# A field step between us and h in units 2 to 21, four more units with the second product in halves, and another order of w_out's splits

## The chip, the cores and the metric

The kernel runs on one core of one Trainium2 chip. The metric is the device time of one execution, in microseconds (us), of which the median over the runs is given. Engines are named as in the profile: PE is TensorE's matmuls and PEld its weight loads, DVE is VectorE, ACT ScalarE, POOL GpSimd, SP SyncE (here the queue that issues DMAs).

## What is computed

```python
X = np.fft.fft(np.fft.fft(x, axis=1), axis=2).real     # x: (8, 3008, 256), float32
h = X.reshape(24064, 256) @ w_in                        # w_in: (256, 2048)
g = np.where(h >= 1, h, np.where(h <= -1, 0.0, (h + 1) ** 2 / 4))
out = g @ w_out                                         # w_out: (2048, 256)
```

The weights arrive as 64-bit floats and are made into float32 on the chip.

## The kernel before

**Units.** The second axis of the transform is folded into w_in, so that the rest is two matrix products with the function g between them. They are cut into 384 units: a batch (8), a chunk of columns (3, of 482, 512 and 512 columns) and 128 of the 2048 hidden features. Each unit carries two signs, since a column and its mirror image come from the same two products. Batch 0 runs its first four features for all three chunks (units 0 to 11), and then the other twelve, chunk by chunk. Units 12 to 23 are features 4 to 15 of the first chunk, 482 columns wide.

**One unit i.** `gemm1(i)` puts six matmuls into two banks `uv` (line 552; three banks in all). DVE adds a correction to the first, giving `us` (line 555). It then writes the difference and the sum with the second bank into a tile `h` (lines 558 and 559, tag `h`, four buffers). ACT makes `a` from `h` (lines 564 and 565). One iteration later `activate` has DVE make g from `a` and `h` (line 574 or 579), and some iterations later `gemm2` multiplies it into four `acc` banks (line 635). From unit 12 on, `gemm2(i)` stands in iteration i + 4.

**Native units and units in halves.** Units below `NATIVE` keep g as one float32 tile in the tag `gh`, and `gemm2` takes four float32 products of it with `wo32` (eight matmul records in the trace, since each product is recorded as two). From `NATIVE` on, g is written over `h`, ACT copies it to a rounded tile `gh` (line 582), and POOL subtracts the two into `gl` (line 598, two instructions, one for each sign). `gemm2` then takes three products per bank, twelve in all, with w_out's high half `woh` and low half `wol`. `low_halves(i)` issues `gl` at the end of iteration i + 2. The first of its two instructions waits for the DVE instruction whose name stands in `after[1]`: the last g, or the last low half of w_out on DVE if one was issued since. In units of this kind the tile `h` is read until `gl` is done.

**The conversions.** Sixteen pieces of the weights (0 to 15) are converted between the units. The step names are: A takes the mantissa field (line 253) and B the exponent field (line 258), both on DVE, and `a` is the two together; b is three ACT instructions (lines 267 to 269); c is two DVE instructions (lines 274 and 275); d is a multiplication on POOL (line 289). Pieces 2, 3, 6, 7, 10, 11, 14 and 15 are w_out's q = 0 to 7, two features each. u takes the high half of one q on ACT (line 300); O takes its low half on DVE (line 304) and Q on POOL. Of the rest, s is the low half of w_in (DVE, lines 363 and 368), f its folding on PE, L loads a part of batch 1's x, and Y folds one on POOL (line 153). A conversion works in a tile of two fields whose tag `WORK` gives, `h` where it names none. Tiles of one tag share its buffers: a new tile takes one only when all readers of an older tile are done.

**Order.** `AHEAD[i]` names steps between `us` and `h` of unit i, `AMID[i]` steps behind `h`, and `STEPS[i]` steps at the end of iteration i (before `gemm2`, if they stand ahead of a "|"). In iterations 0 to 23 `pin()` fixes the order of every engine to the order of the program, so that an instruction that waits holds up everything behind it on its engine. Iterations 22 and 23 hold the first two column sums of batch 1 on PE (`stage1`), which read what Y0 and Y1 have folded.

Of the kernel before, what the change touches and what calls it, by code (L numbers as in the profile page):

```python
# [11 lines left out]
U32 = mybir.dt.uint32  # L12
# [10 lines left out]
P = 128  # L23
# [5 lines left out]
CH = 512  # L29
# [12 lines left out]
def _constants():  # L42
# [36 lines left out]
)  # L79
AHEAD = {1: "v2 G0"}  # L80
AMID = {0: "p11", 1: "p12 D1 E1 q11 q12", 3: "p13 q13", 6: "p14 q14", 7: "f2", 11: "f4", 16: "f6"}
STEPS = {
    0: "c2",
    1: "b3",
    2: "c3 d3",
    3: "a4 b4",
    4: "a5 c4 d4 b5",
    5: "c5 d5",
    7: "f3 a8 s2 b8",
    8: "s3 r1 a9 c8 d8 b9",  # L90
    9: "a6 c9 d9 b6",
    10: "c6 d6",
    11: "f5 a12 s4 b12",
    12: "s5 r2 a13 c12 d12 b13",
    13: "a7 c13 d13 b7",
    14: "c7 d7 u0",
    15: "a10 b10 L0 L1 u1 Q0",
    16: "s6 u2 Q1 |",
    17: "f7 a11 c10 d10 b11",
    18: "s7 r3 c11 d11 L2",  # L100
    19: "a14 Y0 b14 L3 u3 O2",
    20: "a15 c14 d14 b15",
    21: "O3 c15 d15 u4",
    22: "O4 Y1 u6 u5",
    23: "O6 O5 u7",
    24: "O7",
    32: "h",
}

RAW = {0: "gh", 1: "gh", 2: "woh", 3: "woh", 4: "woh", 5: "woh", 6: "wol", 7: "wol", 8: "wol", 9: "wol"}  # L110
RAW |= {10: "xt", 11: "xt", 12: "xt", 13: "xt", 14: "pqh", 15: "pql"}
WORK = {1: "a", 3: "a", 4: "gl", 5: "gl", 7: "a", 8: "gl", 9: "gl", 11: "a", 12: "gl", 13: "gl", 15: "a"}
BUFS = {"h": 4, "a": 3, "gl": 4}

EARLY_BANKS = 12
BANK = {"s2_0_3": "acc3", "delta_1": "acc2"}
FIRST = 4
NATIVE = 20
PINNED = 24
SPARE = (3, 5)  # L120
NEXT = 22
# [5 lines left out]
def fft_ffn_kernel(ctx: ExitStack, tc: tile.TileContext, x, xn, cst, w_in, w_out, out):  # L127
# [3 lines left out]
    sb = ctx.enter_context(tc.tile_pool(name="sb", bufs=1))  # L131
# [3 lines left out]
    xt, yt, zt, nyb, pq = {}, {}, {}, {}, {}  # L135
# [90 lines left out]
    raws, f32s, wo32, shared = {}, {}, {}, {}  # L226
# [20 lines left out]
    def convert_mantissa(n):  # L247
        raw = raws.pop(n)
        tag = WORK.get(n, "h")
        t = sb.tile([P, 2, CH], U32, tag=tag, name=f"cv_{n}", bufs=BUFS[tag])  # L250
        high = raw[:, :, 1]
        cv[n] = t, raw
        nc.vector.tensor_scalar(t[:, 0], high, 0xFFFFF, None, op0=ALU.bitwise_and)  # L253
# [6 lines left out]
    def convert_fields(n):  # L260
        convert_mantissa(n)
        convert_exponent(n)
# [14 lines left out]
    def convert_scale(n, eng):  # L277
        t, _ = cv.pop(n)
        kind, q, *_ = jobs[n]
        man, exp = (t[:, i].bitcast(F32) for i in range(2))  # L280
        dst = man
        if kind == "in":
            f32s[n] = man
        else:
            if q % 2 == 0:
                pair = sb.tile([P, 2, CH], F32, tag="gl", name=f"wo_{q // 2}", bufs=4)
                wo32[q], wo32[q + 1] = pair[:, 0], pair[:, 1]
            dst = wo32[q]
        eng.tensor_tensor(dst, man, exp, op=ALU.mult)  # L289

    wo = {}
# [78 lines left out]
    s1, s2, zn = {}, {}, {}  # L370
# [172 lines left out]
    def gemm1(i):  # L543
# [11 lines left out]
        nc.vector.scalar_tensor_tensor(us, nyb[b, k][:, :n], delta[:, f : f + 1], uv[0], op0=ALU.mult, op1=ALU.add)  # L555
        run_steps(AHEAD.get(i, ""))
        h = sb.tile([P, 2, CH], F32, tag="h", name=f"h_{i}", bufs=4)[:, :, :n]
# [11 lines left out]
    def activate(i):  # L569
        n = WIDTH[units[i][1]]  # L570
        h, a = fronts.pop(i)
        if i < NATIVE:
            g = sb.tile([P, 2, CH], F32, tag="gh", name=f"g_{i}", bufs=4)[:, :, :n]
# [38 lines left out]
    def gemm2(i):  # L612
# [8 lines left out]
        for dh in range(2):  # L621
# [4 lines left out]
            for sg in range(2):  # L626
                acc = accs[dh * 2 + sg]
                if i < NATIVE:
                    wo_at = (f % 2) * D + dh * P
# [45 lines left out]
    def piece_sums(n):  # L675
# [21 lines left out]
        "q": lambda n: stage2_split(0, n - n1 - 1),  # L697
        "a": convert_fields,
        "A": convert_mantissa,
        "B": convert_exponent,  # L700
        "b": convert_floats,
        "c": convert_join,
        "d": lambda n: convert_scale(n, nc.gpsimd),
        "v": lambda n: convert_scale(n, nc.vector),
        "F": lambda n: fold_half(n, 0),
        "f": fold_w_in,
# [13 lines left out]
    def run_steps(names):  # L720
        for s in names.split():
            steps[s[0]](int(s[1:] or 0))
# [17 lines left out]
    for i in range(n_units + LAG):  # L740
# [29 lines left out]
        if i < n_units:  # L770
            run_steps(then)
            change = units[i][2] == (FIRST if b == 0 else 0) + LAG
            while pending and (change or units[i][2] != (FIRST if b == 0 else 0) + LAG - 1 and done < total * (r + 1 - r0) / (per - r0)):
                change = False
                w, f = pending.pop(0)
                f()
                done += w
                n = XC if b + 1 < PLAIN else XT
# [92 lines left out]
```

## Time and profile before

| | us |
|---|---|
| median of 3 runs | 1712.52 |
| lowest and highest of them | 1712.27, 1714.09 |
| the profiled execution | 1712.49 |
| its span, first to last instruction | 1710.7 |

In the profile PE is busy for all but 5.6 us of the span, DVE for 79%, ACT for 78% and POOL for 66% of it. The granted clock of TensorE is full in every slice. The page gives each engine's busy time; the chain of work names what the end of the span hangs on; a timeline lists one engine's instructions in order of time, with the idle time before each in brackets.

### The profile page before, as it was taken

To read this page: it belongs to the slowest core of one execution; us is meant where nothing else is said; L and a number is where in the kernel's file an instruction comes from. 1 tells how busy PE (TensorE), PEld (TensorE's weight loads), DVE (VectorE), ACT (ScalarE), POOL (GpSimd) and SP (SyncE) were. 2 spreads that over 40 slices of the span, in tenths; PEclk is the share of its full clock that TensorE was granted. 3 is DMA by queue.
4 is the path that set the end of the run, shared out by engine and by line. 5 is a ranking of instruction groups with operands and counts; after the bars stand their busy time and mean duration, and the time that the engine had idled before them with its cause. 6 is when DMAs were issued, how large, how long until landed. Compare 5 with 4: busy or idle time off the path is not lost.

```text
span 1710.7 us, 21453 instructions
## 1 busy us (share of the span) xinstructions
PE 1705.1 (100%) x7736; PEld 1389.1 (81%) x7736; DVE 1353.6 (79%) x1762; ACT 1335.6 (78%) x1541; POOL 1123.2 (66%) x921
## 2 busy tenths in 40 slices
PE   9999999999999999999999999999999999999999
PEld 6557888888888888888888888888888888888887
DVE  8998788877777787777777778777777777778776
ACT  6878777877788777887787877887778877777775
POOL 1125678856887568865688657886577855566664
PEclk9999999999999999999999999999999999999999
DMA  8123111100011000110010100101001010000000
GB/s 322 48 98 109 59 57 56 61 13 31 25 45 60 20 25 25 56 48 20 25 62 20 59 8 25 62 24 56 19 13 62 1 36 31 1 25 24 1 25 25
DMA packets 35466, 76.29 MB, mean 45 GB/s; under 512 B 4640, under 2 KB 13344, under 8 KB 35360
## 3 DMA queue, kind: packets, MB, share of 16 engines
q1 hardware_dynamic: 35180, 74.79, 12.6%
q8 instruction: 61, 1.00, 0.2%
q14 instruction: 45, 0.37, 0.1%
q10 hardware_dynamic: 180, 0.14, 0.0%
HBM read 47.10 MB, written 27.81 MB: 44 GB/s over the span
## 4 chain that ended last, share of the span: by engine, by line
PE 99%; DMA 0%; DVE 0%; SPq 0%; ACT 0%; issue 0%
PE acc L635 62%; PE uv L552 31%; PE s L509 3%; PE s L391 2%; PE s L396 1%; PE wps L342 1%; DMA raw<-in_moe_w_in_dram 0%; PE delta L321 0%; PE ny L482 0%; DVE cv L289 0%; DVE o L653 0%; DVE cv L275 0%; DVE y L153 0%; DVE cv L274 0%; DVE o L641 0%; DVE cv L253 0%
## 5 line engine op out<-in xcount | busy, mean ns | idle before, releaser
L598 POOL TENSOR_TENSOR gl<-h,gh 128x512 fp32r<-128x512 f32 (+1 forms) x724 | 908.9, 1276 | 449.2 <-PE acc L635 220.2
L564 ACT ACTIVATE a<-h,biases 128x1024 f32<-128x1024 f32 (+1 forms) x385 | 436.0, 1133 | 265.6 <-DVE h L559 264.1
L635 PE MATMUL acc<-gh,woh 128*128 128x512 f32 (+1 forms) x1456 | 574.3, 394 | 0.0
L635 PE MATMUL acc<-gl,woh 128*128 128x512 f32 (+1 forms) x1456 | 570.0, 391 | 0.0
L635 PE MATMUL acc<-gh,wol 128*128 128x512 f32 (+1 forms) x1456 | 566.9, 389 | 0.0
L555 DVE SCALAR_TENSOR_TENSOR us<-nyb,delta,uv 128x512 f32<-128x512 f32 (+1 forms) x384 | 282.9, 737 | 287.9 <-PE uv L552 287.3
L579 DVE SCALAR_TENSOR_TENSOR h<-a,h 128x1024 f32<-128x1024 f32 (+1 forms) x365 | 477.2, 1308 | 2.6 <-ACT a L565 2.1
L582 ACT ACTIVATE gh<-h 128x1024 fp32r<-128x1024 f32 (+1 forms) x365 | 379.8, 1040 | 46.6 <-DVE h L579 29.5
L565 ACT ACTIVATE a<-a 128x1024 f32<-128x1024 f32 (+1 forms) x385 | 395.1, 1026 | 1.1
L635 PEld LDWEIGHTS acc<-gl,woh 128*128 128x128 f32 x1456 | 274.3, 188 | 57.1
L635 PEld LDWEIGHTS acc<-gh,wol 128*128 128x128 f32 x1456 | 273.7, 188 | 56.4
L635 PEld LDWEIGHTS acc<-gh,woh 128*128 128x128 f32 x1456 | 273.8, 188 | 53.5
L552 PE MATMUL uv<-pqh,wh 128*128 128x512 f32 (+1 forms) x768 | 306.3, 399 | 0.0
L558 DVE TENSOR_TENSOR h<-us,uv 128x512 f32<-128x512 f32 (+1 forms) x384 | 260.3, 678 | 52.0 <-DVE us L555 1.5
L552 PE MATMUL uv<-pql,wh 128*128 128x512 f32 (+1 forms) x768 | 299.3, 390 | 0.0
L552 PE MATMUL uv<-pqh,wl 128*128 128x512 f32 (+1 forms) x768 | 298.9, 389 | 0.0
L559 DVE TENSOR_TENSOR h<-us,uv 128x512 f32<-128x512 f32 (+1 forms) x384 | 257.5, 671 | 0.0
L552 PEld LDWEIGHTS uv<-pqh,wl 128*128 128x128 f32 x768 | 144.2, 188 | 35.0 <-issue 4.6
L552 PEld LDWEIGHTS uv<-pqh,wh 128*128 128x128 f32 x768 | 144.2, 188 | 33.4 <-issue 3.6
L552 PEld LDWEIGHTS uv<-pql,wh 128*128 128x128 f32 x768 | 144.1, 188 | 30.2 <-DVE pql L220 0.4
L166 POOL TENSOR_TENSOR x<-x 120x256 f32<-120x256 f32 x72 | 68.2, 948 | 4.6 <-DVE h L579 3.5
L635 PE MATMUL acc<-g,wo 128*128 128x482 f32 (+1 forms) x160 | 69.6, 577 | 0.0
(80 smaller groups left out, 783.5 us busy)
## 6 DMA issues: line engine op xcount, KB each, us to landing
x<-in_xn_dram SPq DMA_DIRECT2D x36, 512.0 KB, 3.5
out_dram<-o SPq DMA_DIRECT2D x26, 512.0 KB, 2.8
x<-in_x_dram SPq DMA_DIRECT2D x16, 512.0 KB, 6.1
out_dram<-o SPq DMA_DIRECT2D x14, 482.0 KB, 2.9
nyb<-nyr SPq DMA_DIRECT2D x24, 256.0 KB, 3.2
raw<-in_moe_w_in_dram SPq DMA_DIRECT2D x4, 512.0 KB
raw<-in_moe_w_out_dram SPq DMA_DIRECT2D x4, 512.0 KB, 10.5
part<-o SPq DMA_DIRECT2D x4, 512.0 KB, 3.0
```

The costliest lines, as they stand in the source:

```text
L166: return nc.gpsimd.tensor_tensor(t[:, r], t[:, r], t[:, r + 1], op=ALU.add).ins
L509: nc.tensor.matmul(pt[:, i], z[:, c], rm, start=True, stop=True)
L552: nc.tensor.matmul(t[:, :n], w[m][:, cols], r[:, m, :n], start=(j == 0), stop=(j == 2))
L555: nc.vector.scalar_tensor_tensor(us, nyb[b, k][:, :n], delta[:, f : f + 1], uv[0], op0=ALU.mult, op1=ALU.add)
L558: nc.vector.tensor_tensor(h[:, 0], us, uv[1], op=ALU.subtract)
L559: last_h = nc.vector.tensor_tensor(h[:, 1], us, uv[1], op=ALU.add).ins
L564: nc.scalar.activation(a[:, sg], h[:, sg], AF.Relu, bias=half, scale=0.5)
L565: nc.scalar.activation(a[:, sg], a[:, sg], AF.Square)
L579: g = nc.vector.scalar_tensor_tensor(h[:, sg], a[:, sg], 1.0, h[:, sg], op0=ALU.min, op1=ALU.max).ins
L582: nc.scalar.activation(gh[:, sg], h[:, sg], AF.Copy)
L598: ins = nc.gpsimd.tensor_tensor(gl[:, sg], h[:, sg], gh[:, sg].bitcast(F32), op=ALU.subtract).ins
L635: nc.tensor.matmul(acc[:, :n], w, g[:, sg], start=(begin and j == 0), stop=(last and j == len(terms) - 1))
```

## The change

`AHEAD` gets one field step (A or B) for 18 of the units 2 to 21, between `us` and `h`; these steps stood in pairs at the ends of iterations. `NATIVE` falls from 20 to 16, so that units 16 to 19 (features 8 to 11) take three products per bank instead of one. These features need q = 4 and 5 of w_out in halves, so O4 stands in iteration 18 and O5 in 20 (before 22 and 23), O6 in 22 and O7 in 24, and O2 and O3 move behind them, to 25 and 26. Q0 moves from iteration 15 to 14 and Q1 from 16 to 15. For q = 4 to 7, `wo32` is no longer a tile of its own in the tag `gl` but the conversion's own tile, which is thus read until u and O of that q are done. The conversions' tiles move: pieces 9, 12 and 13 share the tag `z`, 10 takes `xt`, 14 takes `a`, and 11 and 15, now named in no entry, take `h`.

```diff
-AHEAD = {1: "v2 G0"}
+AHEAD = {
+    1: "v2 G0",
+    2: "A4",
+    3: "B4",
+    4: "A5",
+    5: "A8",
+    6: "B8",
+    7: "A9",
+    8: "B9",
+    9: "A6",
+    10: "A7",
+    11: "A12",
+    12: "A13",
+    13: "B13",
+    14: "A10",
+    15: "A11",
+    16: "B11",
+    17: "A14",
+    18: "B14",
+    21: "A15",
+}
 STEPS = {
...
-    15: "a10 b10 L0 L1 u1 Q0",
-    16: "s6 u2 Q1 |",
-    17: "f7 a11 c10 d10 b11",
-    18: "s7 r3 c11 d11 L2",
-    19: "a14 Y0 b14 L3 u3 O2",
-    20: "a15 c14 d14 b15",
-    21: "O3 c15 d15 u4",
-    22: "O4 Y1 u6 u5",
-    23: "O6 O5 u7",
-    24: "O7",
+    14: "c13 d13 Q0 B10 u1",
+    15: "b10 L0 Q1",
+    16: "s6 c10 d10 |",
+    17: "f7 b11 u4 L1",
+    18: "s7 r3 c11 d11 O4 L2",
+    19: "Y0 b14 u5 L3",
+    20: "c14 d14 O5",
+    21: "B15 b15 u6",
+    22: "c15 d15 O6 Y1",
+    23: "u7",
+    24: "O7 u2",
+    25: "O2 u3",
+    26: "O3",
...
-WORK = {1: "a", 3: "a", 4: "gl", 5: "gl", 7: "a", 8: "gl", 9: "gl", 11: "a", 12: "gl", 13: "gl", 15: "a"}
-BUFS = {"h": 4, "a": 3, "gl": 4}
+WORK = {1: "a", 3: "a", 4: "gl", 5: "gl", 7: "a", 8: "gl", 9: "z", 10: "xt", 12: "z", 13: "z", 14: "a"}
+BUFS = {"h": 4, "a": 3, "gl": 4, "xt": 4}
...
-NATIVE = 20
+NATIVE = 16
...
+        if tag == "z":
+            if tag not in shared:
+                shared[tag] = sb.tile([P, 3, 2, CH], U32, tag=tag, name="cv_z", bufs=1), iter(range(3))
+            t, slots = shared[tag]
+            t = t[:, next(slots)]
...
-        else:
+        elif q < 4:
...
+        else:
+            wo32[q] = man
```

## Rows read from the trace of the kernel before

**Rows 1.** The page: its head, its part 1, its chain by engine.

```profile
span 1710.7 us, 21453 instructions
...
PE 1705.1 (100%) x7736; PEld 1389.1 (81%) x7736; DVE 1353.6 (79%) x1762; ACT 1335.6 (78%) x1541; POOL 1123.2 (66%) x921
...
PE 99%; DMA 0%; DVE 0%; SPq 0%; ACT 0%; issue 0%
```

**Rows 2.** The chain in order of time, 100 to 180 us: start, duration, what.

```profile
121.44 3.23 PE acc L635 x8
124.68 1.31 PE uv L552 x6
...
133.77 0.87 PE s L396 x8
...
139.44 0.86 PE s L396 x8
...
141.72 2.62 PE acc L635 x12
```

**Rows 3.** DVE's timeline: start, duration, instruction, count, [idle before]; units 1 and 19.

```profile
28.87 0.71 DVE L555 SCALAR_TENSOR_TENSOR us<-nyb,delta,uv 128x482 f32<-128x482 f32 x1
29.50 0.69 DVE L289 TENSOR_TENSOR wo<-cv 128x512 f32<-128x512 f32 x1
...
119.66 0.42 DVE L253 TENSOR_SCALAR cv<-raw 128x512 uint32<-128x512 uint32 x1
```

**Rows 4.** DVE's timeline, from us of unit 18 to us of unit 19.

```profile
111.73 0.72 DVE L555 SCALAR_TENSOR_TENSOR us<-nyb,delta,uv 128x482 f32<-128x482 f32 x1 [1.28 <-PE uv L552]
112.56 0.66 DVE L558 TENSOR_TENSOR h<-us,uv 128x482 f32<-128x482 f32 x1
...
113.70 1.16 DVE L574 SCALAR_TENSOR_TENSOR g<-a,h 128x964 f32<-128x964 f32 x1
114.77 0.75 DVE L363 SCALAR_TENSOR_TENSOR wl<-wps,biases,wh 128x512 fp32r<-128x512 f32 x1
115.43 0.68 DVE L274 SCALAR_TENSOR_TENSOR cv<-raw,cv 128x512 f32<-128x512 uint32 x1
...
116.63 0.71 DVE L555 SCALAR_TENSOR_TENSOR us<-nyb,delta,uv 128x482 f32<-128x482 f32 x1
```

**Rows 5.** DVE's timeline: O4, and h and g in iterations 23 and 24.

```profile
133.70 0.69 DVE L304 TENSOR_TENSOR wol<-wo,woh 128x512 fp32r<-128x512 f32 x1
...
136.44 0.66 DVE L558 TENSOR_TENSOR h<-us,uv 128x482 f32<-128x482 f32 x1
...
137.58 1.54 DVE L579 SCALAR_TENSOR_TENSOR h<-a,h 128x964 f32<-128x964 f32 x1
...
141.95 0.69 DVE L558 TENSOR_TENSOR h<-us,uv 128x512 f32<-128x512 f32 x1
...
143.15 1.95 DVE L579 SCALAR_TENSOR_TENSOR h<-a,h 128x964 f32<-128x964 f32 x1
```

**Rows 6.** POOL's timeline: d11, the two instructions of Y0, Y1, gl of units 20, 21.

```profile
116.80 1.26 POOL L289 TENSOR_TENSOR wo<-cv 128x512 f32<-128x512 f32 x1 [4.89 <-DVE cv L275]
120.62 1.54 POOL L153 TENSOR_TENSOR y<-x 96x512 f32<-96x512 f32 x1 [2.56 <-DVE cv L258]
122.24 0.46 POOL L158 TENSOR_TENSOR x<-x 96x128 f32<-96x128 f32 x1
...
134.46 1.29 POOL L153 TENSOR_TENSOR x<-x 96x512 f32<-96x512 f32 x1 [2.36 <-DVE wol L304]
135.72 2.38 POOL L598 TENSOR_TENSOR gl<-h,gh 128x482 fp32r<-128x482 f32 x2
...
141.66 2.42 POOL L598 TENSOR_TENSOR gl<-h,gh 128x482 fp32r<-128x482 f32 x2
```

**Rows 7.** DVE's timeline: g of unit 2; under it PE's: its second product.

```profile
40.30 1.15 DVE L574 SCALAR_TENSOR_TENSOR g<-a,h 128x964 f32<-128x964 f32 x1
...
41.59 3.47 PE L635 MATMUL acc<-g,wo 128*128 128x482 f32 x8
```

More of the change, by code (lines that the diff above doesn't have):

```diff
@@ L85 @@
     2: "c3 d3",
-    3: "a4 b4",
-    4: "a5 c4 d4 b5",
+    3: "b4",
+    4: "B5 c4 d4 b5",
     5: "c5 d5",
[L89 to L96, printed above, removed]
-    15: "a10 b10 L0 L1 u1 Q0",
-    16: "s6 u2 Q1 |",
-    17: "f7 a11 c10 d10 b11",
-    18: "s7 r3 c11 d11 L2",
-    19: "a14 Y0 b14 L3 u3 O2",
-    20: "a15 c14 d14 b15",
-    21: "O3 c15 d15 u4",
-    22: "O4 Y1 u6 u5",
-    23: "O6 O5 u7",
-    24: "O7",
+    7: "f3 s2 b8",
+    8: "s3 r1 c8 d8 b9",
+    9: "c9 d9 B6 b6",
+    10: "c6 d6 B7",
+    11: "f5 s4 B12 b7",
+    12: "s5 r2 c7 d7 b12",
+    13: "c12 d12 b13 u0",
+    14: "c13 d13 Q0 B10 u1",
[11 more added lines that the diff above has]
+    26: "O3",
     32: "h",
@@ L249, in convert_mantissa @@
         tag = WORK.get(n, "h")
-        t = sb.tile([P, 2, CH], U32, tag=tag, name=f"cv_{n}", bufs=BUFS[tag])
+        if tag == "z":
[4 more added lines that the diff above has]
+        else:
+            t = sb.tile([P, 2, CH], U32, tag=tag, name=f"cv_{n}", bufs=BUFS[tag])
         high = raw[:, :, 1]
@@ L288, in convert_scale @@
             dst = wo32[q]
+        else:
+            wo32[q] = man
         eng.tensor_tensor(dst, man, exp, op=ALU.mult)
```

## The prediction

> **What bounds the kernel now.** I read the page first: PE is busy for 1705.1 of 1710.7 us, and the chain that ends last is PE for 99% [rows 1]. So only what PE executes, or what makes it wait, can move the end, and time that PE loses in the middle doesn't come back. The chain in order of time then shows how PE spends a unit of 482 columns: 1.31 us for the first product, 3.23 us for a native second product, 2.62 us for one in halves [rows 2]. Last I read DVE's timeline in iterations 2 to 25, where the change lies. DVE has hardly a gap there either: in unit 18 it waits once for PE, 1.28 us, and then runs without a pause to the us of unit 19 [rows 4]. So PE is full, DVE is nearly full, and POOL has room between its conversions [rows 6].
>
> **What the change removes on PE.** Units 16 to 19 go from 3.23 to 2.62 us [rows 2]: 4 x 0.61 = 2.44 us less. Nothing else leaves PE. If all stays fed, the time falls by 0.14%.
> The Trainium skill (FP8 and Floating Point Precision, TensorE Precision Notes) gives a true float32 product four passes through the array. By that, a native unit would be 16 passes against 12, and at 2.62 / 12 = 0.218 us a pass the four units would give 4 x 4 x 0.218 = 3.5 us. The rows show 3.7 passes instead of 4, and the sum goes by them.
>
> **What a field step between us and h does.** An instruction that reads us starts 0.83 us behind it [rows 4]; one that doesn't starts 0.63 us behind it [rows 3]. A field step lasts 0.42 us [rows 3]; less the 0.08 us by which two independent instructions overlap there (28.87 + 0.71 against 29.50), it takes 0.34 from start to start. It fills the gap of 0.2 us: h comes 0.63 + 0.34 - 0.83 = 0.14 us later, and the end of the iteration 0.2 us earlier. In early units g is what PE waits for: g of unit 2 ends at 41.45 and its product starts at 41.59 [rows 7]. A4 and B4 delay it by two such steps, so PE loses 0.3 us there (0 to 0.4). From iteration 4 on the native units have more room, and DVE, 0.2 us per unit ahead, comes to unit 18 in time; it waits for PE there today [rows 4], and will again.
>
> **What units in halves add.** Per unit: g is written over h, ACT copies gh, POOL takes two gl instructions, 2.38 us [rows 6]. ACT and POOL, 78% and 66% busy [rows 1], have the time; DVE's g costs the same unless gl runs beside it (below). What matters is which tiles this holds. h of a native unit is free after its g, one iteration on; h of a unit in halves only when gl is done, two iterations on. The tag h has four buffers. From unit 16 on three of them are h(i-1), h(i-2) and h(i-3). The fourth was free in the kernel before. In the changed one it isn't: piece 11 has no entry in WORK, so it takes an h buffer at A11 (iteration 15) and keeps it until O5 (iteration 20), because wo32 of q = 5 is now the conversion's own tile. Piece 15 takes it over at A15 (21) and keeps it until O7 (24). So h(i) must wait for gl(i-3) for i = 19 to 24, instead of gl(i-4). Behind a waiting h stand, in fixed order, DVE's own sum, g, c and O, and so ACT's a, the next gl, and PE's next products.
> No row of before shows an h that waits so; the rows show how near it is. h of unit 23 is written at 136.44, gl of unit 20 ends at 138.10; h of unit 24 at 141.95, gl of unit 21 ends at 144.08 [rows 5, 6]. With one buffer less these would have been late by 1.7 and 2.1 us, and each delay would have moved the next gl as well.
>
> **The chain with the hold, step by step.** Durations: h pair 1.14 us, g 1.07, wl 0.66, each half of c 0.60, O 0.69 (0.60 from start to start) [rows 4, 5]; d 1.26, Y0 2.08 from first start to last end, Y1 1.29, gl 2.38 [rows 6]; 0.05 to 0.1 us for a wait on another engine. Until unit 18 all stands as before (plus the 0.3 us).
> Iteration 18: us 111.73 [rows 4], B14, h 112.70, g 113.84, wl 114.91, c11 to 116.85, O4 ends at 117.45. POOL: d11 to 118.2, then gl(16) to 120.6.
> Iteration 19: us 117.4, h waits until 120.65 (2.4 us idle), g of unit 18 ends at 122.95. Y0 stands behind that g and ahead of gl on POOL: Y0 to 125.1, gl(17) to 127.5.
> Iteration 20: us 122.9, h at 127.55, g, c14, O5 ends at 131.65; d14 to 132.4, gl(18) to 134.8.
> Iteration 21: us, A15, h at 134.85, g ends at 137.15; gl(19) to 139.6.
> Iteration 22: h at 139.65, g, c15, O6 ends at 143.75; d15 to 144.5, Y1 to 145.8, gl(20) to 148.2.
> Iteration 23: h at 148.25, g ends at 150.55, Y2 to 151.9, gl(21) to 154.3.
> Iteration 24: h at 154.35, g, O7 ends at 157.3. Piece 15 is gone, and h of unit 25 no longer waits.
> That is about 6 us a unit, where PE without waits takes 3.9 to 4.9.
>
> PE against it. Without waits its second products would start at 121.3, 125.2, 129.2 and 134.2 for units 16 to 19. It then waits: for gl(17), 1.3 us (its second half is needed at the sixth of twelve matmuls); for a bank, since the second product of gemm1(22) writes where us of unit 21 (131.6 to 132.3) reads, 2.6 us; for gl(18), 0.6; in iteration 23 for Y1 (145.8), which the column sums read, 4.4; then in iterations 25 to 27 for us of units 25 and 26 and for gl(21) to gl(23), together 3.1. Sum 12.0 us. One delay of DVE is charged once here: each wait is counted after PE has moved by those before it.
>
> **Sum.** -2.44 + 0.3 + 12.0 = +9.9 us on the profiled execution's 1712.49, whose span is 1710.7 with 1.8 us around it; its time is that of the median (1712.52). Forecast 1722.4 us, 0.6% slower. Where the stall goes: PE is late for good, DVE then waits for PE again.
>
> **Bounds of what isn't seen.** The waits on h: 0 if my reading of the buffers is wrong (then 1710.4), 4.5 us if only piece 11's hold (iterations 19 and 20) counts (1714.9), 12.0 with both. I take the last, since the rows 1.7 and 2.1 us late lie in just such iterations. After iteration 27 DVE may still trail: 0 to +2 us. Contention: g beside gl took 1.54 and 1.95 us instead of 1.16 [rows 4, 5]. In the chain gl runs while DVE waits, so I take none; 0.8 us in each of six iterations would be +4.8 at most. L1 is issued two iterations later, in 17 (xt is held by piece 10 until c13 and c10 have freed a place): Y1 reads it in 22, five iterations or over 20 us on, so nothing.
>
> **The rivals.**
> First, not slower: the hold doesn't reach PE. PE runs four iterations behind g, and us may trail by some 2.6 us before a bank is late. If h gets a buffer in time (a tile freed earlier than I read), DVE stays at its 4.8 us of work in iteration 20 against PE's 3.9, makes it up in 21, and all that is left is -2.44 + 0.3: 1710.4 us, within 0.2% (some 3.4 us, about what a measurement of this kernel can tell from no change). It decides where h of unit 19 starts before gl(16) ends. For it: g of unit 17 ends at 114.86 [rows 4] and its product starts at 121.44 + 3.23 + 1.31 = 125.98 [rows 2], 11 us of room. Against: that room is g's, not h's.
> Second, half of it: piece 15's hold is harmless, since by then PE is so late that DVE catches up. Only the 4.5 us up to gl(18) stay: 1714.9.
> Third, contention: the hold as above, and g stretched as in [rows 5]: 1727.2. The Trainium skill (SBUF — State Buffer, Who interferes with whom) lets the one of VectorE and GpSimd that starts first keep the shared port for its whole instruction; by that rule every two-input step on DVE beside gl could be held. The trace agrees that g is stretched there, by 0.38 and 0.79 us.
> Fourth, the field step doesn't fill the gap: then DVE has 18 x 0.2 = 3.6 us more to do than I say, and its 1.28 us of waiting in unit 18 takes up a part: 2.3 us more, 1724.7.
>
> **Chances.** The forecast, with the fourth rival and what trails in iterations 28 on: 0.70 (1717 to 1728). Second rival 0.10, one half of it slower by over 0.2%. First rival 0.13. Contention beyond 1728: 0.04. Faster by over 0.2%: 0.03, since 2.44 us is all that PE can gain. So slower 0.79, within 0.2% 0.18, faster 0.03. The range reaches over the second rival, 1713.5 to 1728, and leaves out the first (0.13) and the far ends.
>
> **What would show it.** In the changed profile: second products of 2.6 us from unit 16 on; a field step 0.63 us behind us and h 0.97 behind it; h of units 19 to 24 with idle time of 2 to 4 us before it, ended by POOL's gl; PE idle before the column sums of iteration 23, and behind DVE's us in iteration 22. I am wrong if DVE shows no gaps before h in iterations 19 to 24, or if they are there and PE shows none.

## The result: 14.0 us slower, and the profile after

| | before | after |
|---|---|---|
| median of 4 runs, us | 1712.49 | 1726.53 |
| lowest and highest | 1712.27, 1714.09 | 1726.18, 1726.84 |
| the profiled execution | 1712.49 | 1726.41 |
| its span | 1710.7 | 1724.6 |

The ratio is 1.008, with a 95% interval from 1.0062 to 1.0097. The direction and the range of the forecast (1722.4, from 1713.5 to 1728) held; the middle was 4.1 us too low. Line numbers are 30 higher than before: us is L585, h L588 and L589, g L604 or L609, gl L628, the second product L665.

The page of the changed kernel: head, part 1, the granted clock in 40 slices, and the group of the first of the two h instructions.

```profile
span 1724.6 us, 21498 instructions
...
PE 1709.1 (99%) x7752; PEld 1394.0 (81%) x7752; DVE 1357.5 (79%) x1762; ACT 1339.1 (78%) x1545; POOL 1136.3 (66%) x929
...
PEclk9998999999999999999999999999999999999999
...
L588 DVE TENSOR_TENSOR h<-us,uv 128x512 f32<-128x512 f32 (+1 forms) x384 | 260.1, 677 | 61.7 <-POOL gl L628 13.9
```

PE was idle for 5.6 us of the span before [rows 1]; now it is idle for 15.5, and it is "busy" 4 us more although it has less to do. In one slice of the clock it doesn't run at full speed. And h has a new releaser: 13.9 us of idle time ended by gl on POOL.

**Where PE loses it.** For each unit I take the start of its first matmul, less that of unit 0, and compare with the same in the kernel before. This number, PE's lateness, is the measure below; it is needed because on the chips of the later runs some executions, of the kernel before too, begin unit 0 up to 5 us later (the profiled ones of free_h, pool_memset and pool_to20 by 4.7 to 4.8), which their times contain and their lateness doesn't. The last column stays as it is to the end of the span.

| PE's lateness in us at unit | 6 | 17 | 21 | 23 | 25 | 40 |
|---|---|---|---|---|---|---|
| changed kernel | 1.06 | 2.99 | 2.76 | 7.56 | 13.42 | 13.43 |

So 3.0 us are gone by unit 17, ahead of anything that the units in halves do, and 10.4 more go in units 21 to 25. With the 2.44 us that PE saves, the second loss is 13.43 - 2.99 + 2.44 = 12.9 us. The whole loss stands in the first tenth of the kernel.

**The second loss.** DVE's timeline of the changed kernel, h of units 19 to 23, and one g among them:

```profile
124.59 0.66 DVE L588 TENSOR_TENSOR h<-us,uv 128x482 f32<-128x482 f32 x1 [2.90 <-POOL gl L628]
...
125.73 1.16 DVE L609 SCALAR_TENSOR_TENSOR h<-a,h 128x964 f32<-128x964 f32 x1
...
131.22 0.66 DVE L588 TENSOR_TENSOR h<-us,uv 128x482 f32<-128x482 f32 x1 [3.71 <-POOL gl L628]
...
139.03 0.66 DVE L588 TENSOR_TENSOR h<-us,uv 128x482 f32<-128x482 f32 x1 [2.28 <-POOL gl L628]
...
143.96 0.66 DVE L588 TENSOR_TENSOR h<-us,uv 128x482 f32<-128x482 f32 x1 [1.68 <-POOL gl L628]
...
153.23 0.66 DVE L588 TENSOR_TENSOR h<-us,uv 128x482 f32<-128x482 f32 x1 [2.83 <-POOL gl L628]
```

PE's timeline there: what it waited for, and the second column sums.

```profile
130.06 0.49 PE L665 MATMUL acc<-gl,woh 128*128 128x482 f32 x1 [1.13 <-POOL gl L628]
...
136.01 0.49 PE L582 MATMUL uv<-pqh,wh 128*128 128x482 f32 x1 [2.32 <-DVE us L585]
...
148.75 0.50 PE L582 MATMUL uv<-pqh,wh 128*128 128x512 f32 x1 [1.39 <-DVE us L585]
...
152.08 0.77 PE L665 MATMUL acc<-gl,woh 128*128 128x482 f32 x1 [2.15 <-POOL gl L628]
...
154.65 1.86 PE L426 MATMUL s<-cs,x 96*128 96x96 f32 x8
```

Each of these h waits, and PE waits behind it: for a bank that a late us still reads, and for gl. The windows of the same kernel add what PE does after such a wait. Columns: the stretch, its length, busy time and count of PE, PEld, DVE, ACT and POOL, the granted clock as a share of full speed, DMA share, GB/s.

```profile
135.00:140.00 5.00, 3.93 (x10) 2.71 (x11) 2.72 (x5) 0.53 (x1) 3.99 (x3) 0.67 0.00 0
...
150.00:155.00 5.00, 2.92 (x8) 2.38 (x9) 2.17 (x4) 0.80 (x2) 3.20 (x3) 0.54 0.00 0
155.00:160.00 5.00, 5.00 (x23) 4.41 (x22) 1.99 (x4) 4.32 (x8) 3.65 (x3) 0.78 0.34 108
```

The granted clock is full up to there. Behind the idle 2.32 us and again with the idle 2.15 us it falls, so part of these stretches runs at 1.2 instead of 2.4 GHz: products start 0.40 instead of 0.22 us apart. The eight products from 136.81 took 3.51 us where 8 x 0.218 = 1.74 is usual; nine products and one group of column sums (0.81 us at full clock) from 152.08 took 5.33 instead of 2.77. That is 4.3 us, on top of 7.25 us of marked idle time (the four waits above and one of 0.26). Together 11.6 of the 12.9. From start to start each of the five waits costs PE some 0.17 us more than its mark, 0.8 us in all; I have not placed the last 0.5.

### The profile page after: what moved, and what is told of

Its sections match the earlier page's. It is cut to its first block, busy times and chain, and to the rows that moved or that the text cites. A ratio compares the mean times of both kernels' runs of the same rounds, so it can differ in the third digit from the quotient of the medians.

```text
span 1724.6 us, 21498 instructions
## 1 busy us (share of the span) xinstructions
PE 1709.1 (99%) x7752; PEld 1394.0 (81%) x7752; DVE 1357.5 (79%) x1762; ACT 1339.1 (78%) x1545; POOL 1136.3 (66%) x929
## 4 chain that ended last, share of the span: by engine, by line
PE 91%; DVE 5%; issue 1%; POOL 1%; ACT 0%; SPq 0%; DVEq 0%; POOLq 0%
PE acc L665 58%; PE uv L582 28%; PE s L539 2%; PE s L421 2%; DVE g L604 1%; DVE h L589 1%; DVE us L585 1%; DVE h L588 1%; POOL gl L628 1%; PE s L426 0%; DVE cv L303 0%; DVE cv L302 0%; DVE o L683 0%; DVE h L609 0%; POOL cv L319 0%
## 5 line engine op out<-in xcount | busy, mean ns | idle before, releaser
L628 POOL TENSOR_TENSOR gl<-h,gh 128x512 fp32r<-128x512 f32 (+1 forms) x732 | 920.6, 1279 | 450.6 <-PE acc L665 233.3
L665 PE MATMUL acc<-gh,woh 128*128 128x512 f32 (+1 forms) x1472 | 581.8, 395 | 0.0
L665 PE MATMUL acc<-gl,woh 128*128 128x512 f32 (+1 forms) x1472 | 577.9, 393 | 3.6 <-POOL gl L628 3.5
L665 PE MATMUL acc<-gh,wol 128*128 128x512 f32 (+1 forms) x1472 | 574.0, 390 | 0.0
L585 DVE SCALAR_TENSOR_TENSOR us<-nyb,delta,uv 128x512 f32<-128x512 f32 (+1 forms) x384 | 282.9, 737 | 287.3 <-PE uv L582 286.9
L609 DVE SCALAR_TENSOR_TENSOR h<-a,h 128x1024 f32<-128x1024 f32 (+1 forms) x369 | 480.0, 1301 | 3.2 <-ACT a L595 2.5
L612 ACT ACTIVATE gh<-h 128x1024 fp32r<-128x1024 f32 (+1 forms) x369 | 383.8, 1040 | 44.9 <-DVE h L609 28.5
L665 PEld LDWEIGHTS acc<-gl,woh 128*128 128x128 f32 x1472 | 277.9, 189 | 63.5 <-POOL gl L628 6.0
L665 PEld LDWEIGHTS acc<-gh,wol 128*128 128x128 f32 x1472 | 277.5, 189 | 57.1
L665 PEld LDWEIGHTS acc<-gh,woh 128*128 128x128 f32 x1472 | 277.5, 189 | 53.8
L588 DVE TENSOR_TENSOR h<-us,uv 128x512 f32<-128x512 f32 (+1 forms) x384 | 260.1, 677 | 61.7 <-POOL gl L628 13.9
L589 DVE TENSOR_TENSOR h<-us,uv 128x512 f32<-128x512 f32 (+1 forms) x384 | 257.7, 671 | 0.0
L199 POOL TENSOR_TENSOR x<-x 120x256 f32<-120x256 f32 (+1 forms) x42 | 61.9, 1475 | 2.9 <-DVE h L609 2.5
```

What stands on the lines that cost most here:

```text
L199: return nc.gpsimd.tensor_tensor(t[:, 3], t[:, 0], t[:, 2], op=ALU.subtract).ins
L588: nc.vector.tensor_tensor(h[:, 0], us, uv[1], op=ALU.subtract)
L589: last_h = nc.vector.tensor_tensor(h[:, 1], us, uv[1], op=ALU.add).ins
L609: g = nc.vector.scalar_tensor_tensor(h[:, sg], a[:, sg], 1.0, h[:, sg], op0=ALU.min, op1=ALU.max).ins
L612: nc.scalar.activation(gh[:, sg], h[:, sg], AF.Copy)
L628: ins = nc.gpsimd.tensor_tensor(gl[:, sg], h[:, sg], gh[:, sg].bitcast(F32), op=ALU.subtract).ins
```

## The experiments

Lateness as above. Each ratio is to the kernel before on the same chip; three kernels were run once and have none. The last column is the part of the lateness that went on slower matmuls: what they took from start to start, where the granted clock was below full, above the same matmuls at full clock.

| kernel | median us | ratio, 95% interval | 6 | 17 | 23 | 25 | 40 | slower matmuls |
|---|---|---|---|---|---|---|---|---|
| changed | 1726.53 | 1.008 [1.0062, 1.0097] | 1.06 | 2.99 | 7.56 | 13.42 | 13.43 | 4.3 |
| free_15 | 1726.70 | 1.0069 [1.0054, 1.0084] | 1.06 | 2.96 | 7.01 | 13.39 | 13.38 | 2.1 |
| free_h | 1725.96 | 1.0058 [1.0039, 1.0077] | 1.06 | 3.00 | 5.26 | 10.59 | 10.59 | 3.4 |
| pairs | 1724.89 | 1.0058 [1.0043, 1.0073] | 0.02 | 1.88 | 6.64 | 11.95 | 12.75 | 3.3 |
| free_pairs | 1720.63 | 1.0036 [1.0022, 1.0049] | 0.01 | 1.89 | 4.34 | 7.65 | 7.65 | 0 |
| free_pairs_v | 1720.97 | 1.0048 [1.0033, 1.0063] | 0.00 | 1.86 | 2.81 | 6.43 | 6.42 | 0 |
| native18 | 1717.74 | 1.0033 [1.0020, 1.0046] | 0.00 | 1.86 | 1.24 | 6.28 | 6.28 | 3.3 |
| native20 | 1719.20 | 1.0042 [1.0028, 1.0056] | 1.05 | 2.99 | 2.99 | 4.72 | 6.75 | 0 |
| b4_early | 1726.17 | one run | 0.49 | 2.35 | 7.35 | 13.10 | 13.20 | 4.6 |
| before_hold | 1718.46 | 1.0031 [1.0018, 1.0044] | -0.01 | -0.01 | -0.01 | -0.01 | 7.46 | 2.9 |
| before_pool | 1722.30 | 1.0064 [1.0042, 1.0086] | 0.02 | 0.02 | 0.58 | 7.61 | 7.61 | 3.2 |
| pool_memset | 1717.94 | one run | 0.01 | 0.01 | 0.01 | 0.59 | 0.59 | 0 |
| pool_to20 | 1724.74 | one run | 0.03 | 0.03 | 0.58 | 7.59 | 7.59 | 3.2 |

The lateness of two kernels can therefore be near each other for different reasons: before_pool's 7.6 us and before_hold's 7.5 hold some 3 us of slower matmuls each, free_pairs' 7.65 none. Windows of before_pool and of before_hold, with columns as above:

```profile
145.00:150.00 5.00, 5.00 (x15) 4.07 (x14) 4.19 (x6) 3.76 (x8) 3.77 (x4) 0.50 0.35 105
```

```profile
165.00:170.00 5.00, 5.00 (x14) 3.85 (x13) 4.41 (x7) 3.87 (x7) 2.53 (x2) 0.50 0.85 273
```

### Is it the hold of the h buffers?

**free_h** writes the finished float32 weights of pieces 11 and 15 into the raw data's tile, so that their working tile gives its h buffer back after d; L3 moves to iteration 20.

```diff
+        elif q in (5, 7):
+            dst = raw.rearrange("p e two -> p (e two)")[:, :CH].bitcast(F32)
+            wo32[q] = dst
         else:
             wo32[q] = man
```

> The changed kernel, but the finished pieces 11 and 15 (q = 5 and 7 of w_out) are written into the tiles of their raw data, so that their conversion tiles give back the h buffers at d11 and d15; L3 moves from iteration 19 to 20, since raw piece 11 now keeps its xt buffer until O5. Theory, the hold: the waits of h on gl in iterations 19 to 24 (2.90, 3.71, 2.28, 1.68 and 2.83 us in the changed kernel) go, and the granted clock stays full, since PE no longer idles there. What is left is the 3.0 us that PE has lost before unit 18, less 2.4 for the units in halves: 1713.1 us (1712 to 1715). Rival, too much work: four more units in halves load POOL and DVE so that gl is late whatever buffer h gets: above 1720, with PE still waiting for gl of units 17 to 20.

Only 2.8 of 13.4 us came back, 0.9 of them through the clock. The hold alone is not the cause: with the buffer free, other things are late. DVE's timeline of free_h (g beside gl, then the first half of c beside Y0's end and gl):

```profile
128.03 2.22 DVE L612 SCALAR_TENSOR_TENSOR h<-a,h 128x964 f32<-128x964 f32 x1
...
133.70 3.29 DVE L302 SCALAR_TENSOR_TENSOR cv<-raw,cv 128x512 f32<-128x512 uint32 x1
```

They take 1.16 and 0.68 us alone. h of units 19, 20 and 23 hardly waits any more. h of units 21 and 22 waits as before (2.29 and 1.68 us): piece 15's working tile still takes an h buffer at A15, just in front of h of unit 21, and has it until d15 in iteration 22. So this run lifts the hold in part; free_pairs, below, leaves one h that waits for gl, by 1.11 us.

**free_15** does the same for piece 15 alone (`elif q in (7,)`).

> The changed kernel, but only piece 15 (q = 7) is written into its raw data's tile; piece 11 still keeps an h buffer until O5, and piece 15 keeps one only until d15 in iteration 22. Theory, the hold: h of units 19 to 22 still wait for gl, those of 23 and 24 don't. PE's waits for gl(17), gl(18) and for us of unit 21 stay (some 4.7 us at full clock), those for gl(20) and behind it go: 1718 to 1722. If the hold of piece 15 is harmless: 1726 as before. If all the loss is in piece 15's: about 1713.

Nothing came back (13.38 against 13.43). h of unit 23 no longer waits for gl, but DVE's g now runs beside gl of unit 20, whose two instructions take 3.36 us instead of 2.37, and PE waits 2.66 us for its first half instead of 2.15.

### The field steps

**pairs** is the changed kernel with the field steps back in pairs at the ends of iterations, and the hold left as it is.

```diff
-AHEAD = {1: "v2 G0", 2: "A4", 3: "B4", ...}
+AHEAD = {1: "v2 G0"}
 STEPS = {
-    3: "b4",
-    4: "B5 c4 d4 b5",
+    3: "a4 b4",
+    4: "a5 c4 d4 b5",
...
-    15: "b10 L0 Q1",
+    15: "a10 b10 L0 Q1",
```

> The changed kernel with the field steps put back as pairs at the ends of the iterations (ahead of their b), all else as changed, the hold too. Theory: nine of the eighteen field steps between us and h took 0.84 to 1.20 us instead of 0.42, each beside a multiplication on POOL that had started within the us before it, and two of these delays reach PE (1.1 us before the second product of unit 2 and 1.1 inside the first product of unit 12, some 0.8 in iteration 16 and 17). So 3.0 us go and the hold stays: 1723.5 (1722 to 1725). Rival: the field step between us and h is worth its place and the 3.0 us come from the new order of the conversions: 1726 or more.

The early loss is gone (0.02 at unit 6, 0.07 at unit 16), so 2.2 us of it came from the field steps between us and h. But 1.8 us are lost anew in iteration 16: PE waits 0.33 us for us and 0.95 for a copy of `acc`. DVE is late there, and not by the steps put back. O2 and O3 stand in iterations 25 and 26 of the program, where `pin()` no longer fixes the order, and in the trace they run far ahead of that: in iteration 17 in the changed kernel (114.13 and 114.73), and here between us and h of units 13 and 14, beside d. DVE's timeline of pairs:

```profile
87.92 1.38 DVE L314 TENSOR_TENSOR wol<-wo,woh 128x512 fp32r<-128x512 f32 x1
...
93.94 1.38 DVE L314 TENSOR_TENSOR wol<-wo,woh 128x512 fp32r<-128x512 f32 x1
```

From us of unit 13 to us of unit 16 DVE takes 16.8 us here and 14.1 before: the difference is the length of these two. The same two rows, and 1.9 us at unit 17, come back in free_pairs, free_pairs_v and native18. So these kernels differ from the changed one in more than the steps, and the 1.8 us can't be given to the steps' place. At the end 0.7 us of the 3.0 are won.

**b4_early** moves one of these steps: B4 behind A4 in unit 2, where POOL has nothing to do.

```diff
-    2: "A4",
-    3: "B4",
+    2: "A4 B4",
```

> The changed kernel with B4 moved from unit 3 to unit 2, behind A4, so that it lies where POOL has no multiplication running. Theory (a field step is blocked by POOL's multiplication that started before it): B4 takes 0.42 us instead of 1.20, and PE waits about 0.5 us instead of 1.1 before the second product of unit 2 or a later one of the first units. Rival (it is slow because of where it stands behind us, whatever POOL does): B4 takes about 1 us beside an idle POOL. The time stays near 1726 us, since the rest is as changed.

DVE's timeline of the changed kernel (B4 in unit 3) and under it POOL's:

```profile
37.91 0.72 DVE L585 SCALAR_TENSOR_TENSOR us<-nyb,delta,uv 128x482 f32<-128x482 f32 x1
38.54 1.20 DVE L286 TENSOR_SCALAR cv<-raw_woh 128x512 uint32<-128x512 uint32 x1
39.66 0.64 DVE L588 TENSOR_TENSOR h<-us,uv 128x482 f32<-128x482 f32 x1
```

```profile
38.18 1.27 POOL L319 TENSOR_TENSOR wo<-cv 128x512 f32<-128x512 f32 x1 [20.30 <-DVE cv L303]
```

DVE's timeline of b4_early, the same step:

```profile
34.48 0.43 DVE L285 TENSOR_SCALAR cv<-raw_woh 128x512 uint32<-128x512 uint32 x1
```

B4 takes 0.43 us where POOL is idle and 1.20 where a multiplication on POOL began 0.36 us before it. PE's lateness at unit 6 falls from 1.06 to 0.49, as expected. In the changed kernel 12 of the 18 field steps between us and h took 0.84 to 1.20 us, each beside a multiplication or Q on POOL (the expectation of pairs counted nine); the six with POOL idle took 0.41 or 0.42. At the end only 0.2 of the 0.64 us won by unit 20 is left: an early loss is partly paid out of the later waits.

### Does POOL slow DVE down by itself?

**before_pool** is the kernel before with two subtractions on POOL, of the shape of gl, at the ends of iterations 18 to 21. Nobody reads them, and no h buffer is held.

```diff
+        for sg in range(2):
+            ins = nc.gpsimd.tensor_tensor(
+                extra[0][:, sg, :n], wh[0][:, :n].bitcast(F32), wh[1][:, :n].bitcast(F32), op=ALU.subtract
+            ).ins
```

> The kernel before, with two subtractions on POOL added at the ends of each of the iterations 18 to 21: the shape of gl, two SBUF inputs, the first of a pair behind DVE's last instruction as gl is. They read w_in's folded parts and write a scratch tile that nobody reads, so no buffer is held and nothing waits for them. Theory, the port: POOL's instructions and DVE's that read two SBUF operands (g, c, O) exclude each other, so these 8 x 1.2 us come out of DVE's time, which has no room there; PE loses 4 to 6 us: 1717 to 1719. Theory, the hold: only held h tiles and results that come late cost PE time: 1712 to 1713.

It cost 7.6 us. DVE's timeline of before_pool (g, the mantissa step, g, O), and POOL's:

```profile
118.34 1.67 DVE L574 SCALAR_TENSOR_TENSOR g<-a,h 128x964 f32<-128x964 f32 x1
119.94 1.46 DVE L253 TENSOR_SCALAR cv<-raw 128x512 uint32<-128x512 uint32 x1
...
124.20 3.18 DVE L574 SCALAR_TENSOR_TENSOR g<-a,h 128x964 f32<-128x964 f32 x1
...
132.78 1.70 DVE L304 TENSOR_TENSOR wol<-wo,woh 128x512 fp32r<-128x512 f32 x1
```

```profile
123.96 2.40 POOL L690 TENSOR_TENSOR extra<-wh,wh 128x482 f32<-128x482 f32 x2
...
130.63 3.29 POOL L690 TENSOR_TENSOR extra<-wh,wh 128x482 f32<-128x482 f32 x2
```

Against 1.16 for g, 0.42 for the step and 0.69 for O [rows 3 to 5], these four and one more g (1.73) are 5.2 us longer. PE's marked waits are 0.29, 0.49 and 2.94 us, the last in front of the second column sums, and 3.2 us went on matmuls at the lower clock behind it. POOL's longer queue could have done this too: the fold for the column sums and gl(20) stand behind the extra work, and the profile puts the end of the 2.94 us down to gl. So two more.

**pool_memset** puts five memsets in the place of the two subtractions.

```diff
-        for sg in range(2):
-            ins = nc.gpsimd.tensor_tensor(...)
+        for sg in range(5):
+            ins = nc.gpsimd.memset(extra[0][:, sg % 2, :n], 0.0).ins
```

> The kernel before with five memsets of 128x482 on POOL at the ends of iterations 18 to 21, in place of the two extra subtractions there: about as long on POOL (0.52 us each by the row of the one memset of before), but they read nothing. Theory (an extra subtraction costs because DVE's instructions with two operands wait beside it): no g, c or O is longer than 1.2 us beside a memset, and PE is late by under 3 us behind iteration 25 instead of the 7.6 with the subtractions. Rival (POOL's queue is what costs: gl and the folds behind the extra work come later): again about 7 us. If DVE is stretched beside memsets too, the two are not told apart.

**pool_to20** leaves out the extra work of iteration 21.

```diff
-    21: "O3 c15 d15 u4 I",
+    21: "O3 c15 d15 u4",
```

> The kernel before with the two extra subtractions on POOL at the ends of iterations 18, 19 and 20 alone, not 21, so that POOL's queue is empty again before the fold and gl of unit 20 in iteration 22. Theory (DVE is stretched beside them): g, field steps and O are stretched by some 4 us up to iteration 21, and PE is late by 3 to 6 us behind iteration 25. Rival (POOL's queue): under 1.5 us.

POOL's timeline of pool_memset, and DVE's beside it (g, then the mantissa step; the first O):

```profile
127.89 2.26 POOL L690 MEMSET extra<- 128x482 f32 x5
...
133.32 2.27 POOL L690 MEMSET extra<- 128x482 f32 x5
```

```profile
128.15 1.16 DVE L574 SCALAR_TENSOR_TENSOR g<-a,h 128x964 f32<-128x964 f32 x1
129.23 1.21 DVE L253 TENSOR_SCALAR cv<-raw 128x512 uint32<-128x512 uint32 x1
...
134.91 0.68 DVE L304 TENSOR_TENSOR wol<-wo,woh 128x512 fp32r<-128x512 f32 x1
```

With POOL about as long at work (2.26 us against 2.40, or 3.3 where the subtractions were stretched themselves), g and O beside the memsets keep their 1.16 and 0.68 us, and PE is late by 0.59 instead of 7.61 us. Without the work of iteration 21 the loss is the same 7.59, DVE is stretched by the same 5.2 us, and PE waits the same 2.94 us. ACT's and PE's timelines of pool_to20, at the end of that wait:

```profile
146.97 1.33 ACT L439 ACTIVATE z<-s 64x192 f32<-64x192 f32 x4
```

```profile
148.40 2.00 PE L396 MATMUL s<-cs,x 96*128 96x96 f32 x8 [2.94 <-issue]
```

Here gl's first half had ended 1.6 us before PE went on, so gl was not what PE waited for. In both kernels PE starts 0.10 us behind ACT's last copy of the first column sums (`z`), out of the one bank that both groups of column sums use; and ACT was late because it had stood idle for 2.9 us until DVE wrote h of unit 22. So it isn't POOL's queue; it is DVE's instructions with two operands in SBUF that wait beside POOL's subtractions. us and h, which read one operand from a PE bank, keep their lengths in both. A field step waits beside the memsets too (1.21 here, 0.88 an iteration before).

The Trainium skill (SBUF — State Buffer, SBUF: two separate sides) says just this: VectorE and GpSimd share one pair of ports as an exclusive lock, and what asks for it on VectorE is an instruction in a two-port mode, or one with two SBUF inputs, the latter only against a GpSimd instruction that reads SBUF. By that rule the field step, if it runs in such a mode (512 elements in 0.42 us, where h takes 0.66 for 482), should be held by memsets and g not, and the rows agree: 1.21 against 0.42 us, and 1.16 against 1.16.

### Does the hold cost anything by itself?

**before_hold** is the kernel before with one h buffer taken by a tile that two short ACT writes keep from iteration 18 to 26.

```diff
+    def hold():
+        held.append(sb.tile([P, 2, CH], F32, tag="h", name="held", bufs=4))
+        nc.scalar.activation(held[0][:, 0, :1], half, AF.Copy)
```

> The kernel before, with one tile of the tag h taken from the end of iteration 18 to the end of iteration 26 (two ACT instructions on one column write it; nobody else does). The units in halves begin at 20 as before, so h of units 23 to 26 has three buffers left. Theory, the hold: h of unit 23 waits 1.7 us for gl of unit 20, the next ones some 2 us each, and PE loses 3 us (2 to 5): 1715.5. Theory, the port: the wait only takes the place of DVE's standing still beside gl, and the kernel loses under 1 us.

It does: 7.5 us, over twice what I expected, of which 2.9 went on slower matmuls (PE's marked waits sum to 3.4 us). No g up to 170 us is longer than 1.16 us (1.23 with 1024 columns), so this is the hold without the contention. DVE's timeline of before_hold, two of the five h that wait, and PE's:

```profile
138.03 0.66 DVE L559 TENSOR_TENSOR h<-us,uv 128x482 f32<-128x482 f32 x1 [1.88 <-POOL gl L599]
...
145.31 0.69 DVE L559 TENSOR_TENSOR h<-us,uv 128x512 f32<-128x512 f32 x1 [3.12 <-POOL gl L599]
```

```profile
154.59 0.50 PE L553 MATMUL uv<-pqh,wh 128*128 128x512 f32 x1 [0.77 <-DVE us L556]
...
163.87 0.77 PE L636 MATMUL acc<-gh,woh 128*128 128x512 f32 x1 [1.50 <-DVE os L650]
```

These are h of units 23 and 24, the two that the prediction called late by 1.7 and 2.1 us with a buffer less [rows 5, 6]. PE's loss shows only at units 28 to 30 (2.1, 7.1, 7.5 us), when it has used up its distance.

### Both undone, and fewer units in halves

**free_pairs** is pairs and free_h together.

> The two together: no hold of h by pieces 11 and 15, field steps as pairs at the ends of iterations. Theory: what is left of the change is 4 x 0.61 us on PE: 1710.1 (1709.5 to 1711), faster than the kernel before by 0.14%. Rival: without the steps between us and h DVE lacks 0.2 us a unit and comes late to the units in halves: 1713 or more.

Expected was a time at or below the kernel before; it is 7.65 us late, with the granted clock full. 1.9 of it are lost by unit 17, as in pairs. DVE's timeline of free_pairs (g of units 18 and 19) and POOL's (gl):

```profile
121.29 2.20 DVE L592 SCALAR_TENSOR_TENSOR h<-a,h 128x964 f32<-128x964 f32 x1
...
126.06 3.78 DVE L592 SCALAR_TENSOR_TENSOR h<-a,h 128x964 f32<-128x964 f32 x1
```

```profile
120.08 2.39 POOL L611 TENSOR_TENSOR gl<-h,gh 128x482 fp32r<-128x482 f32 x2
...
126.40 2.42 POOL L611 TENSOR_TENSOR gl<-h,gh 128x482 fp32r<-128x482 f32 x2
```

Hardly any h waits for gl now. Instead g, 1.16 us long in the changed kernel (its row at 125.73 above), is 2.20 and 3.78 us long, because DVE now works while gl and the folds run. These two, a third g and two field steps up to 139 us are 6.0 us longer than alone; the rival's 0.2 us a unit would have been 3.6 at most.

**free_pairs_v** takes POOL's multiplications d11, d14 and d15 to DVE (`v11`, `v14`, `v15` in STEPS), so that POOL has gl and folds alone.

> The version without the hold and with field steps as pairs, with the multiplications of pieces 11, 14 and 15 on DVE instead of POOL (in iterations 18, 20 and 22). Theory, the port: each takes 0.69 us of DVE instead of 1.27 to 1.66 us in which DVE's two-operand instructions stand, and gl starts earlier: 2 to 3 us less than that version's 1720.6: 1718. Rival, DVE's own work is the bound: three instructions more, 1722.

The trace shows 1.2 us less lateness (6.42), about half of what I expected; the medians, 1720.63 and 1720.97, show none. DVE's own work grew, and PE now waits 0.87 us for a low half of w_out.

**native18** is free_pairs with units 16 and 17 native again.

```diff
-NATIVE = 16
+NATIVE = 18
```

> The version without the hold and with field steps as pairs, with only units 18 and 19 added to the units in halves (16 and 17 stay native; L2 moves to iteration 20 and L3 to 21, since piece 10's tile is read until unit 17's product). Theory, the port: four instructions of gl less, 4.8 us of the port, against 1.2 us more on PE: 3 to 4 us less than 1720.6: 1717. Rival, the order of the splits and of batch 1's loads costs the time: 1720 or more.

As expected in time, though 3.3 of the 6.28 us of lateness are slower matmuls that the sum did not have. By unit 23 PE is only 1.24 us late; then it waits 2.20 us for a fold that stands behind d15 on POOL, and does the column sums at the lower clock (2.02 instead of 1.03 us).

**native20** is the changed kernel with units 16 to 19 native, and wo32 of q = 4 and 5 a tile of its own again.

```diff
-NATIVE = 16
+NATIVE = 20
...
-        elif q < 4:
+        elif q < 6:
```

> The changed kernel with units 16 to 19 native again: NATIVE 20 instead of 16, and wo32 of q = 4 and 5 a tile of its own again, so piece 11 gives its h buffer back at d11 (iteration 18). Field steps, the order of w_out's splits and piece 15's hold of an h buffer (21 to 24) stay as changed. Theory (the eight extra gl, with what they hold and what they stretch on DVE, are the larger part): the 2.44 us of the halves go back to PE, the 3.0 us of the field steps stay (PE late by about 3 at unit 17), piece 15's hold costs h of units 23 and 24 at most 3 us: 1715.5 to 1718. Rival (the order of conversions and splits itself costs): 1722 or more, with PE waits in iterations 18 to 22 and no gl among what ends them.

It was 1.2 us above the range that I gave. Between units 17 and 23 PE loses nothing: 2.99 stays 2.99, so the other order of splits and conversions costs nothing up to there. The other 3.8 us are not piece 15's hold alone. DVE's timeline of native20, O5 and h of unit 23, and PE's:

```profile
128.68 2.98 DVE L334 TENSOR_TENSOR wol<-wo,woh 128x512 fp32r<-128x512 f32 x1
...
144.76 0.66 DVE L588 TENSOR_TENSOR h<-us,uv 128x482 f32<-128x482 f32 x1 [4.08 <-POOL gl L628]
```

```profile
143.88 1.10 PE L426 MATMUL s<-cs,x 96*128 96x96 f32 x8 [1.50 <-POOL gl L628]
```

The profile puts the 1.50 us down to gl, whose first half ended 0.31 us before; but ACT's last copy of the first column sums ended 0.10 us before, as in before_pool. ACT had been idle for 4.16 us until h of unit 21, which stood behind the O5 above: 2.98 us, 0.68 alone, beside a fold and d14. So the first 1.7 us (unit 24: 4.72) go back to that contention, were lost before h of unit 23 was written, and come with the place of O5 in the new order. How much of the last 2.0 us is piece 15's hold was not separated.

So units 16 to 19 in halves cost 13.43 - 6.75 = 6.7 us net in the changed kernel, 9.1 us without the saving on PE; 4.3 of these are the slower matmuls. None of the kernels is faster than the one before.

## Why the prediction came close, and where it went wrong

**The saving on PE** (2.44 us) is right. In the changed kernel the second product of unit 16 starts at 124.31 and the next first product at 126.93: 2.62 us.

**The place and the chain of the hold** are right. From one h to the next the forecast was 6.9, 7.3, 4.8 and 8.6 us for units 19 to 23; the rows give 6.63, 7.81, 4.93 and 9.27. h of unit 19 was told to wait 2.4 us and waited 2.90. h of unit 24 did not wait: PE was by then the later one. On PE the 1.3 us for gl(17) were 1.13 and 0.26, the 2.6 us for the bank 2.32; the 0.6 us for gl(18) did not occur. The chain began later than told: us of unit 18 stood at 115.34 instead of 111.73, behind the field steps and behind O2 and O3, which run in iteration 17 and not, as the text above has it, in 25 and 26.

**The sum of 12.0** came out as 12.9, but not by its terms. The 4.4 us for Y1 did not occur. The second column sums, which read Y1, were placed inside the second product of unit 20, and that had waited 2.15 us for gl(20), which stands behind d15 and Y1 on POOL; so Y1 was long done. And 4.3 us went to the lower clock, which the sum did not have: before, PE was hardly ever idle and the clock was full throughout. That the two sizes nearly met is partly luck.

**The field steps** are the term of the sum that was mis-sized: 0.3 us forecast, 2.3 measured at unit 16 and 3.0 at unit 17. The last 0.7 us can't be given to them with certainty, since pairs loses 1.8 us at the same place. "It fills the gap of 0.2 us" holds where POOL is idle: us to step 0.63 us, step to h 0.34 (the undisturbed steps of the changed kernel, such as A4: us 33.55, step 34.17, h 34.51). The step that failed is the duration, 0.42 us from [rows 3]: a row where POOL was idle, used for places where d runs. d follows c, and c stands at the end of an iteration, so a step moved to just behind the next us lands on d, as 11 of 18 did (a twelfth landed on Q). "From iteration 4 on the native units have more room" failed too: PE lost 1.0 us more at unit 12 and 0.7 at 16. The fourth rival had doubts of the same term, but for another reason (a gap not filled) and at less.

**The contention.** "In the chain gl runs while DVE waits, so I take none" is right for the changed kernel: its g in iterations 20 to 24 all take 1.16 us. What was wrong is what I let follow from it. I treated the hold as the one cause, with 1710.4 us if it were lifted. free_pairs lifts it and stays 7.65 us late: 1.9 us by unit 17, with O2 and O3 in iterations 13 and 14, and the rest since DVE then works beside gl and is held there. The two causes take each other's place: the hold makes DVE wait in front of h while gl runs, without the hold it waits inside g, c and O. In the kernel before each of them alone makes PE 7.5 to 7.6 us late (before_hold, before_pool), of which about 3 us are slower matmuls and the rest waits; no row gives a reason why the two come out alike. In the changed kernel the waits on h lead to 12.9 us, 4.3 of them slower matmuls. So neither the 7.5 nor the 12.9 us is a price of the waits alone. The sign was in [rows 5]: g of 1.54 and 1.95 us beside gl. I booked it as a rival of +4.8 us on top of the hold, and did not ask what the first rival's 1710.4 would be with it.

**Open.** What the eight gl would cost without both causes was not tried, since gl has no other engine with room: DVE is itself nearly full. No kernel lifts all of the hold and keeps the field steps where they are, none fixes the place of O2 and O3, and none keeps the clock full beside the same waits, so these shares are not told apart further than above.

## What to carry to other kernels

Before you price a wait, ask what stands behind it: run the sum once more with the wait gone, and see whether the engine then meets the next limit. Take the duration of a moved instruction from a row with the same neighbours on the other engine that it will have in its new place, and look at the longest rows of a group, not only at its mean. And add the clock: an engine that is hardly ever idle has a price for idling that no row of the kernel before shows, and when you compare two experiments by their time, take that price out first.

## What was not expected of the hardware

- A field step of 128x512 on DVE, 0.42 us alone, took 0.84 to 1.20 us beside a multiplication or Q on POOL (1.27 us alone), and 0.88 and 1.21 beside memsets.
- g, 1.16 us alone, took up to 3.78 us beside a fold and gl; the first half of c, 0.68 alone, up to 3.29. Beside memsets g stayed at 1.16.
- After PE had idled 2.3 and 2.2 us, the granted clock was 0.67, 0.54 and 0.78 of full speed in three stretches of 5 us, and 4.3 us went on matmuls that were slower, over half as much as on the waits themselves (7.25). In free_pairs, where PE idled 5.6 us behind unit 17 in waits of at most 1.17 us, the clock stayed full.
